# Re-ordering the steps of a fused linear-attention and rational-MLP kernel: a new table of steps, the same instructions

## The chip, the core and the metric

The kernel runs on one core of a Trainium2 chip. The metric is the device time of one execution in microseconds (us). Engines are named as the profile names them: PE is TensorE, with PEld its weight loads, DVE is VectorE, ACT is ScalarE, POOL is GpSimd, and SP is SyncE, which here only issues DMAs.

## The reference

Two stages are computed one after the other. The first is a gated linear recurrence over 768 time steps for 4 batches of 8 heads with head size 48. The second takes the 3072 x 384 result through a 2048-wide layer with a rational activation.

```python
f = 1.0 / (1.0 + np.exp(-f_logit))
for t in range(S):
    state = f[:, :, t, :, None] * state + np.einsum('bhd,bhe->bhde', k[:, :, t], v[:, :, t])
    y[:, :, t] = np.einsum('bhd,bhde->bhe', q[:, :, t], state)
...
h = x @ w_in
P = a[0] + a[1] * h + a[2] * h2 + a[3] * h3
Q = 1.0 + np.abs(b[0]) * np.abs(h) + np.abs(b[1]) * h2
g = P / (Q + 1e-06)
return (g @ w_out).astype(np.float32)
```

## The kernel before

The work is cut into 12 units, each of 256 time steps of one batch. Unit n belongs to batch n mod 4, so units 0 to 3 start the recurrence of the four batches, and unit n needs the state that unit n - 4 left. Within a unit the recurrence is done in its chunked form with matmuls, and the second stage follows on the unit's 256 tokens.

Every piece of work is a step with a short name. A step issues the instructions of one small function, and the text `ORDER` (lines 19 to 98) lists all 823 steps. The tile framework is in a mode in which it records exactly this order: each engine carries out its own instructions in the order of the text, and semaphores hold an instruction until its inputs are there and its output buffer is free. So the text sets the order within each of the five queues, and nothing else decides it.

The steps that the prediction speaks of, with their engines:

- `ld n f/k/q` loads inputs through SP's queue, and `ld n v` through POOL's (line 193). `wi 8 12` loads columns 8 to 11 (in blocks of 128) of `w_in` through POOL's queue (line 199). `>ls.1` holds a load until step `ls 1` has run.
- `cu`, `ci` build triangular constants and the identity on POOL. `cz`, `cm` clear or build constants on DVE. `fa` works out scale factors from `b` on DVE (from line 247), and `fb` scales `a`.
- `ef`, `ls` (ACT) take exp and log of the gates of a unit. `cs` (PE, line 286) sums them over time. `A` (ACT, line 302) takes exp of the sums, `A n 0` for q and `A n 1` for k. `xa n 0` and `xa n 1` (DVE, line 308) scale q and k with it.
- `T` (PE, line 320) transposes q and k, `Te` (ACT or DVE, line 332) copies the result out. `sc` (PE, line 345) forms the scores of one half of the heads, `mk` (DVE, line 353) masks them. `yb` and `yi` (PE, line 367) form the output `y`, and `ye` (ACT, or DVE for one third of unit 0) copies it into `xT`.
- `kv`, `si` (PE) form the new state, `ae` (ACT) its decay, `st` (DVE, line 445) writes it. `vm` (POOL, line 360) copies parts of v into a padded tile that `yb` needs.
- `h n m0 m1` (PE, line 454) multiplies `xT` with blocks m0 to m1 of `w_in`; `ha` and `hb` are the two parts of such a step. `hy` (ACT, or DVE once) copies the product out as bf16. `sq`, `ab`, `p1`, `p2`, `pm`, `gm` (DVE) and `ln`, `lz`, `ex` (ACT) form the rational function; `u` (PE) or `zd` (an adding DMA from POOL) forms the denominator, `ta` (an adding DMA) or `tv` (DVE) adds up the numerator.
- `o` (PE, line 567) multiplies with `w_out`, `oe` copies out, `so` stores.
- `dz k @s` issues k matmuls on constants (tile `warm`, line 295) whose result is not used; they keep PE busy.

`@s` names one of four PSUM slots of two banks each. Buffers for loads are three deep per input, so a load of unit n waits until the data of the unit three loads earlier has been read.

Of the kernel before, what the change touches and what calls it, by code (L numbers as in the profile page):

```python
# [19 lines left out]
ld 0 f 2 4; cu 1; cz 0; ab_ b a; ld 0 f 0 2; cz 2; ld 0 k 0 2; cu 0; ld 0 k 2 4; ld 0 q 2 4; ci; cm; dz 9 @0  # L20
ld 0 q 0 2; ld 1 f; ld 0 v; ab_ a s; ld 1 k; fa; ld 1 q; ef 0 2 4; ef 0 0 2; cz 3; ls 0 0 2; ls 0 2 4; cz 1
cs 0 2 4 @2; cs 0 0 2 @3; A 0 0 2 4; dz 4 @0; A 0 1 2 4; xa 0 0 2 4; A 0 1 0 2; xa 0 1 2 4; A 0 0 0 2
xa 0 1 0 2; T 0 2 4 @0; vm 0 1; kv 0 @3; Te 0 2 4; wi 8 12; xa 0 0 0 2; ae 0; sc 0 1 @0; si 0 0; mk 0 1
T 0 0 2 @2; ef 1; dz 5 @1; fr; Te 0 0 2; ld 2 f >mk.0.1; ls 1; ld 3 f; st 0 0; sc 0 0 @0; ld 2 k; cs 1 @2
# [5 lines left out]
pm 0 8 16; h 1 12 16 @1; ls 3; st 1 1; hy 0 4 8; p2 0 8 16; h 1 8 12 @0; hy 1 12 16; ab 0 4 8; sq 0 4 8  # L30
h 0 0 4 @2; hy 1 8 12; xa 2 1; ab 1 8 16; h 1 4 8 @3; ld 5 k; hy 0 0 4; ld 4 k; sq 1 8 16; ld 6 f; cs 3 @1
hy 1 4 8; ab 0 0 4; u 0 12 16 @2; xa 2 0; vm 2 0; A 3 1; ld 4 v; p1 0 0 8; T 2 @0; ln 0 12 16; ld 3 v; xa 3 1
u 0 8 12 @3; A 3 0; ta 0 8 16; sq 0 0 4; Te 2 s; h 1 0 4 @2; vm 2 1; xa 3 0; wo 8 12; ln 0 8 12; p2 0 0 8
sc 2 0 @0; kv 2 @1; ef 5; mk 2 0; si 2 0; ae 2; hy 1 0 4; sc 2 1 @3; st 2 0; yb 2 0 2 @0; ex 0 8 16; mk 2 1
# [591 lines left out]
```

## Time and profile before

| what | value |
|---|---|
| runs | 216.26, 216.90, 217.07 us; median 216.9 us |
| span of the profiled execution, first to last instruction | 214.4 us |
| PE busy | 201.0 us (94%) |
| DVE busy | 201.7 us (94%) |
| ACT busy | 195.8 us (91%) |
| POOL busy | 83.7 us (39%) |
| read from and written to HBM | 25.17 MB, 4.72 MB |

The profiled execution shows its span only. The median of the runs stands 2.5 us above that span, and this is taken as what lies around it. In what follows, a row of the timeline starts with the start and the duration in us, and ends with the idle time before it and what ended it. The first and last columns of a table by stretches are the stretch and the DMA rate; between them stand the busy times of the engines.

### The profile page before, as it was taken

To read this page: it belongs to the slowest core of one execution; us is meant where nothing else is said; L and a number is where in the kernel's file an instruction comes from. 1 tells how busy PE (TensorE), PEld (TensorE's weight loads), DVE (VectorE), ACT (ScalarE), POOL (GpSimd) and SP (SyncE) were. 2 spreads that over 40 slices of the span, in tenths; PEclk is the share of its full clock that TensorE was granted. 3 is DMA by queue.
4 is the path that set the end of the run, shared out by engine and by line. 5 is a ranking of instruction groups with operands and counts; after the bars stand their busy time and mean duration, and the time that the engine had idled before them with its cause. 6 is when DMAs were issued, how large, how long until landed. Compare 5 with 4: busy or idle time off the path is not lost.

```text
span 214.4 us, 7128 instructions
## 1 busy us (share of the span) xinstructions
PE 201.0 (94%) x3166; PEld 139.9 (65%) x3166; DVE 201.7 (94%) x213; ACT 195.8 (91%) x204; POOL 83.7 (39%) x93
## 2 busy tenths in 40 slices
PE   5875999899999999999999899999999999999993
PEld 1544587567767686586687587686577676776461
DVE  4786899999999999999999999999999999999991
ACT  3574689999999999999999999999999999999990
POOL 5161009009165072183270496696350603114200
PEclk9999999999999999999999999999999999999999
DMA  5999999999999999999999499999499896988823
GB/s 143 240 257 217 201 242 197 195 223 223 187 200 248 247 235 219 253 228 203 192 292 193 81 294 215 209 225 208 89 192 200 164 196 126 174 282 151 187 84 148
DMA packets 61199, 43.20 MB, mean 202 GB/s; under 512 B 51184, under 2 KB 55024, under 8 KB 61168
## 3 DMA queue, kind: packets, MB, share of 16 engines
q0 software_dynamic: 21520, 23.86, 67.3%
q1 hardware_dynamic: 39360, 18.68, 34.5%
q8 instruction: 25, 0.41, 0.8%
q10 hardware_dynamic: 288, 0.20, 0.3%
q14 instruction: 6, 0.05, 0.1%
HBM read 25.17 MB, written 4.72 MB: 139 GB/s over the span
## 4 chain that ended last, share of the span: by engine, by line
PE 39%; DVE 29%; ACT 14%; DMA 9%; issue 6%; SPq 2%; POOL 1%; DVEq 0%
PE hp L454 13%; PE op L567 12%; DVE gall L557 6%; DMA w_in_sb<-in_moe_w_in_dram 6%; DVE gall L545 4%; ACT qi L527 4%; ACT hy L484 4%; DVE z L497 3%; DVE h L489 3%; DVE scm L353 3%; DMA fn<-in_f_logit_dram 3%; PE u L505 3%; DVE gall L531 3%; PE y L367 2%; DVE hy L536 2%
## 5 line engine op out<-in xcount | busy, mean ns | idle before, releaser
L567 PE MATMUL op<-w_out_sb,gall 128*128 128x384 bf16 x384 | 69.2, 326 | 0.4 <-DVE gall L557 0.4
L454 PE MATMUL hp<-xT,w_in_sb 128*128 128x256 bf16 x564 | 66.7, 273 | 2.1 <-DMA w_in_sb<-in_moe_w_in_dram 2.0
L454 PEld LDWEIGHTS <-w_in_sb 128*128 128x128 bf16 x564 | 54.2, 98 | 11.5 <-DMA w_in_sb<-in_moe_w_in_dram 2.5
L567 PEld LDWEIGHTS <-gall 128*128 128x128 bf16 x384 | 36.1, 98 | 23.6 <-DVE gall L557 0.8
L484 ACT CAST hy<-hp 128x1024 bf16<-128x1024 f32 x47 | 48.1, 1076 | 2.3 <-PE hp L478 1.4
L527 ACT ACTIVATE qi<-lq 128x2048 bf16<-128x2048 f32 (+1 forms) x26 | 48.0, 1861 | 0.1
L360 POOL COPY vmp<-vn 128x128 bf16<-128x128 bf16 x24 | 35.2, 1516 | 28.4 <-DMA vn<-in_v_dram 22.7
L549 POOL DMA_DIRECT2D gall<-hy x20 | 20.0, 1068 | 53.9 <-ACT lsp L276 10.6
L523 ACT ACTIVATE lq<-z 128x2048 f32<-128x2048 bf16 (+1 forms) x20 | 36.8, 1874 | 0.0
L353 DVE TENSOR_TENSOR scm<-sc,mask 128x1024 bf16<-128x1024 f32 x24 | 29.0, 1215 | 1.9 <-PE sc L345 1.7
L489 DVE TENSOR_TENSOR h<-hy 128x4096 bf16<-128x4096 bf16 (+2 forms) x19 | 28.5, 1500 | 0.0
L557 DVE TENSOR_TENSOR gall<-gall,qi 128x4096 bf16<-128x4096 bf16 (+2 forms) x17 | 28.2, 1666 | 0.2
L545 DVE TENSOR_TENSOR gall<-gall,h 128x4096 bf16<-128x4096 bf16 (+2 forms) x17 | 28.1, 1652 | 0.0
L519 POOL DMA_DIRECT2D z<-h x17 | 19.3, 1366 | 17.0 <-PE u L505 6.0
L302 ACT ACTIVATE A<-cs 128x768 f32<-128x768 f32 (+1 forms) x26 | 19.4, 799 | 1.8 <-PE cs L286 1.8
L193 POOL DMA_DIRECT2D vn<-in_v_dram x12 | 12.4, 1030 | 15.7 <-PE y L367 7.9
L531 DVE TENSOR_SCALAR gall<-hy,a_sb 128x4096 bf16<-128x4096 bf16 (+1 forms) x14 | 16.9, 1208 | 0.0
L536 DVE TENSOR_SCALAR hy<-hy,a_sb 128x4096 bf16<-128x4096 bf16 (+1 forms) x14 | 16.6, 1185 | 0.0
L497 DVE TENSOR_SCALAR z<-hy 128x4096 uint16<-128x4096 uint16 (+2 forms) x19 | 15.7, 834 | 0.4 <-ACT hy L484 0.4
L330 ACT COPY qkT<-tp 128x1024 f32<-128x1024 f32 x11 | 11.6, 1058 | 3.2 <-PE tp L320 3.2
L320 PE MATMUL tp<-ident,qkp 128*128 128x128 bf16 x192 | 12.9, 219 | 0.8 <-DVE qkp L308 0.5
L320 PEld LDWEIGHTS <-qkp 128*128 128x128 bf16 x192 | 11.5, 98 | 2.5 <-DVE qkp L308 0.9
(73 smaller groups left out, 255.8 us busy)
## 6 DMA issues: line engine op xcount, KB each, us to landing
gall<-hy POOLq DMA_DIRECT2D x18, 512.0 KB, 7.1
z<-h POOLq DMA_DIRECT2D x15, 512.0 KB, 8.4
fn<-in_f_logit_dram SPq DMA_DIRECT2D x11, 384.0 KB, 8.5
kn<-in_k_dram SPq DMA_DIRECT2D x11, 384.0 KB, 12.1
qn<-in_q_dram SPq DMA_DIRECT2D x11, 384.0 KB, 11.3
out_dram<-osb SPq DMA_DIRECT2D x11, 384.0 KB, 5.1
vn<-in_v_dram POOLq DMA_DIRECT2D x12, 192.0 KB, 8.9
w_in_sb<-in_moe_w_in_dram POOLq DMA_DIRECT2D x4, 384.0 KB, 10.1
```

What stands on the lines that cost most here:

```text
L320: nc.tensor.transpose(t[:, x, i, p, :], s["qk"][:, i, x, 2 * p:2 * p + 2, :].rearrange("t h d -> t (h d)"), ident)
L353: return nc.vector.tensor_mul(t, s["sc", g].rearrange("s r a i t -> s (r a) (i t)"), mb)
L360: nc.gpsimd.tensor_copy(s["vm"][:, :, :, 32 * x:32 * x + 16], src)
L454: nc.tensor.matmul(t[:, m - m0, :], w_in_sb[:, kk, m * P:(m + 1) * P], s["x"][:, kk].rearrange("p i j t -> p (i j t)"), start=(kk == 0), s ...
L484: (nc.scalar.copy if eng == "s" else nc.vector.tensor_copy)(fl(big(s, "hy", "hy", 3), m0, m1), fl(s["hp", m0], 0, m1 - m0))
L489: return nc.vector.tensor_mul(fl(big(s, "h2", "h2", 2), m0, m1), fl(s["hy"], m0, m1), fl(s["hy"], m0, m1))
L523: nc.scalar.activation(fl(lq, m0, m1), fl(s["z"], m0, m1), AF.Ln, scale=regs[2], bias=1.0 + 1e-6)
L527: nc.scalar.activation(fl(qi, m0, m1), fl(lq, m0, m1), AF.Exp, scale=-1.0)
L531: return nc.vector.tensor_scalar(fl(big(s, "g", "gall", 3), m0, m1), fl(s["hy"], m0, m1), a_sb[:, 3:4], a_sb[:, 2:3], op0=ALU.mult, op1=AL ...
L545: return nc.vector.tensor_mul(fl(s["g"], m0, m1), fl(s["g"], m0, m1), fl(s["h2"], m0, m1))
L557: return nc.vector.tensor_mul(fl(s["g"], m0, m1), fl(s["g"], m0, m1), fl(qi, m0, m1))
L567: nc.tensor.matmul(s["op", j][:, j, 0:DM], s["g"][:, m, P * j:P * j + P], w_out_sb[:, m, :], start=(s["on", j] == 1), stop=(s["on", j] == KF))
```

## The change

Only the text `ORDER` changes. Both texts hold the same 823 steps with the same arguments, apart from the PSUM slots behind `@`; nothing is added, taken away or given to another engine. The new text has one line fewer, so every later line of the kernel has a number lower by one. The order is described as found by a search that moves steps within each engine's queue. Two lines of the text show its form; the second pair holds the same place in the work, the first product with `w_in`:

```diff
-ld 0 f 2 4; cu 1; cz 0; ab_ b a; ld 0 f 0 2; cz 2; ld 0 k 0 2; cu 0; ld 0 k 2 4; ld 0 q 2 4; ci; cm; dz 9 @0
+ld 0 f 2 4; ab_ b a; ld 0 f 0 2; ld 0 v; ef 0 2 4; ef 0 0 2; ls 0 0 2; cu 0; ld 0 k 2 4; fa; dz 5 @0; dz 9 @2
...
-Te 1 s; st 0 1; ab 0 8 12; ha 0 12 16 @0; ef 2; sc 1 1 @3; sc 1 0 @1; mk 1 1; ls 2; hb 0 12 16; cs 2 @2; ld 5 f
+sq 0 8 12; ab 0 8 12; ld 2 q; ha 0 12 16 @3; hb 0 12 16; sc 1 0 @0; vm 1 0; mk 1 0; ef 2; ld 2 v; ls 2
```

On PE the steps ahead of the first `cs` were `dz 9` and are now `dz 5` and `dz 9`; the five came later before, behind the second `T` of unit 0. SP's queue now has `ld 1 f` ahead of `ld 0 k 0 2` and `ld 0 q 0 2`, which stood ahead of it.

On DVE the first chain of the program, that of unit 0 up to its first `ye` (the tile `xT`), reads like this before; `qkp0` and `qkp1` are the scaled q and k of units 0 and 1, `scm` the masked scores:

```order
L235 MEMSET vmp1_95 128x8x8
L308 TENSOR_TENSOR qkp0_87<-qn_135,A_89 128x2x4x48
L308 TENSOR_TENSOR qkp0_87<-kn_127,A_89 128x2x4x48 x2
L332 COPY qkT_258<-tp_207 128x4x256
L308 TENSOR_TENSOR qkp0_87<-qn_135,A_89 128x2x4x48
L353 TENSOR_TENSOR scm1_282<-sc_264,mask_85 128x1024
L332 COPY qkT_258<-tp_284 128x4x256
L445 TENSOR_TENSOR state0_1_97<-sv_217,alast_262 128x384
L353 TENSOR_TENSOR scm0_334<-sc_309,mask_85 128x1024
L435 TENSOR_SCALAR xT_426<-y_340,sig_109 128x2x2x64
L308 TENSOR_TENSOR qkp1_88<-kn_161,A_89 128x2x8x48
L308 TENSOR_TENSOR qkp1_88<-qn_172,A_89 128x2x8x48
```

The same place on DVE reads like this in the new order:

```order
L241 MEMSET state3_0_102 128x192
L331 COPY qkT_216<-tp_205 128x4x256
L307 TENSOR_TENSOR qkp0_87<-kn_126,A_89 128x2x4x48
L307 TENSOR_TENSOR qkp0_87<-qn_184,A_89 128x2x4x48
L352 TENSOR_TENSOR scm1_243<-sc_223,mask_85 128x1024
L331 COPY qkT_216<-tp_291 128x4x256
L444 TENSOR_TENSOR state0_1_97<-sv_245,alast_287 128x384
L352 TENSOR_TENSOR scm0_382<-sc_314,mask_85 128x1024
L307 TENSOR_TENSOR qkp1_88<-qn_289,A_89 128x2x8x48
L434 TENSOR_SCALAR xT_419<-y_333,sig_109 128x2x2x64
L444 TENSOR_TENSOR state0_0_96<-sv_245,alast_287 128x384
L307 TENSOR_TENSOR qkp1_88<-kn_301,A_89 128x2x8x48
```

The clearing of the four state tiles (`cz 3`) moved from ahead of the chain to ahead of its first copy, the scaling of unit 1's q (`xa 1 0`) moved ahead of the `xT` row, and the second state of unit 0 (`st 0 1`) now stands right behind that row.

On POOL the first loads of v (`vn`) and of `w_in` stand like this before, with the copies into the padded tiles `vmp0` (even units) and `vmp1` (odd units):

```order
masks.py:199 AFFINE_SELECT ident_84<-ident_84 128x128
L193 DMA vn_158<-in_v_dram 128x8x96
L360 COPY vmp0_94<-vn_158 128x8x16
L199 DMA w_in_sb_110<-in_moe_w_in_dram 128x3x512 x2
L360 COPY vmp0_94<-vn_158 128x8x16
L193 DMA vn_355<-in_v_dram 128x8x96
L199 DMA w_in_sb_110<-in_moe_w_in_dram 128x3x512 x2
L193 DMA vn_445<-in_v_dram 128x8x96
L360 COPY vmp1_95<-vn_355 128x8x16 x2
```

In the new order the same place on POOL reads:

```order
masks.py:199 AFFINE_SELECT ident_84<-ident_84 128x128
L359 COPY vmp0_94<-vn_116 128x8x16 x2
L198 DMA w_in_sb_110<-in_moe_w_in_dram 128x3x512 x2
L192 DMA vn_312<-in_v_dram 128x8x96
L198 DMA w_in_sb_110<-in_moe_w_in_dram 128x3x512
L359 COPY vmp1_95<-vn_312 128x8x16
L198 DMA w_in_sb_110<-in_moe_w_in_dram 128x3x512
L359 COPY vmp1_95<-vn_312 128x8x16
L192 DMA vn_507<-in_v_dram 128x8x96
```

The load of unit 0's v left this place: it is now the first instruction of POOL's program, ahead of all constants. The fourth load of `w_in` (blocks 0 to 3) moved behind a copy that reads unit 1's v, and so does the load of unit 2's v.

More of the change, by code (lines that the diff above doesn't have):

```diff
@@ L19 @@
 ORDER = """
-ld 0 f 2 4; cu 1; cz 0; ab_ b a; ld 0 f 0 2; cz 2; ld 0 k 0 2; cu 0; ld 0 k 2 4; ld 0 q 2 4; ci; cm; dz 9 @0
[L21 to L24, printed above, removed]
@@ L30 @@
[L30 to L34, printed above, removed]
```

142 lines of the change are left out of this document (75 added, 67 removed).

## The prediction

> **What bounds the kernel now.** First I read busy time by stretches, because a mean over the program hides where an engine has room.
>
> ```profile
> core 0: us, PE busy (x) PEld busy (x) DVE busy (x) ACT busy (x) POOL busy (x), PEclk, DMA share, GB/s
> 0.00:25.10 25.10, 17.81 (x314) 10.73 (x314) 17.92 (x47) 13.23 (x21) 9.01 (x23) 1.00 1.15 212
> 25.10:35.00 9.90, 9.64 (x149) 7.74 (x149) 9.36 (x14) 8.61 (x11) 2.32 (x3) 1.00 1.15 225
> 35.00:199.30 164.30, 161.88 (x2639) 114.74 (x2636) 164.24 (x136) 164.01 (x163) 71.52 (x67) 1.00 1.05 204
> 199.30:214.40 15.10, 11.65 (x69) 6.67 (x69) 10.16 (x18) 9.91 (x12) 0.84 (x1) 1.00 0.47 139
> ```
>
> From 35 to 199 us DVE idles 0.06 us of 164.30, ACT 0.29 us and PE 2.42 us. The instructions stay the same, so an order cannot shorten this stretch: it can only put waits into it. All that can be won is DVE's idle time ahead of it, 7.18 us up to 25.1 and 0.54 us up to 35, and what lies in the tail. The tail I leave as it is: the same DVE steps follow `gm 10` in both texts, and so do the 64 matmuls of `o 10` and `o 11`, which with the last `u` fill most of PE's 11.65 us there.
>
> So the second view is the timeline of DVE in the head. The brackets give the idle time before a row and who ended it.
>
> ```profile
> 4.10 0.17 DVE L247 TENSOR_SCALAR bm<-b_sb 128x2 uint32<-128x2 uint32 x1 [0.73 <-DMA b_sb<-in_moe_b_dram]
> ...
> 5.59 0.84 DVE L242 MEMSET state<- 128x192 f32 x4
> ...
> 7.69 0.56 DVE L308 TENSOR_TENSOR qkp<-qn,A 128x384 bf16<-128x384 f32 x1 [0.78 <-ACT A L302]
> ...
> 13.00 1.23 DVE L353 TENSOR_TENSOR scm<-sc,mask 128x1024 bf16<-128x1024 f32 x1
> 14.86 0.48 DVE L435 TENSOR_SCALAR xT<-y,sig 128x256 bf16<-128x256 f32 x1 [0.64 <-PE y L367]
> 15.26 0.95 DVE L308 TENSOR_TENSOR qkp<-kn,A 128x768 bf16<-128x768 f32 x1
> 16.13 0.95 DVE L308 TENSOR_TENSOR qkp<-qn,A 128x768 bf16<-128x768 f32 x1
> 17.00 0.73 DVE L259 TENSOR_SCALAR a_sb<-a_sb,sig 128x3 f32<-128x3 f32 x3
> 18.33 1.23 DVE L484 CAST hy<-hp 128x1024 bf16<-128x1024 f32 x1 [0.60 <-PE hp L454]
> 19.47 0.55 DVE L445 TENSOR_TENSOR state<-sv,alast 128x384 bf16<-128x384 f32 x1
> 19.93 0.42 DVE L497 TENSOR_SCALAR z<-hy 128x1024 uint16<-128x1024 uint16 x1
> 22.09 1.23 DVE L353 TENSOR_TENSOR scm<-sc,mask 128x1024 bf16<-128x1024 f32 x1 [1.74 <-PE sc L345]
> 23.24 0.68 DVE L489 TENSOR_TENSOR h<-hy 128x1024 bf16<-128x1024 bf16 x1
> 23.84 1.22 DVE L353 TENSOR_TENSOR scm<-sc,mask 128x1024 bf16<-128x1024 f32 x1
> ```
>
> DVE waits 0.78 us for the first `A`, 0.64 for the first `y`, 0.60 for the first product with `w_in`, and 1.74 for unit 1's scores. The third view says what those waits hang on: the timeline of PE, and that of POOL, which issues the weights.
>
> ```profile
> 2.67 3.89 PE L295 MATMUL warm<-Ui 128*128 128x512 bf16 x9 [2.67 <-POOL Ui L218]
> 6.64 0.24 PE L286 MATMUL cs<-lsp,Ui 128*128 128x192 bf16 x1
> ...
> 7.30 1.03 PE L295 MATMUL warm<-Ui 128*128 128x512 bf16 x4
> ...
> 16.81 1.48 PE L454 MATMUL hp<-xT,w_in_sb 128*128 128x256 bf16 x12 [1.74 <-DMA w_in_sb<-in_moe_w_in_dram]
> 18.13 1.06 PE L320 MATMUL tp<-ident,qkp 128*128 128x128 bf16 x16
> 21.08 0.61 PE L478 MATMUL hp<-xT,w_in_sb 128*128 128x256 bf16 x4 [1.90 <-DMA w_in_sb<-in_moe_w_in_dram]
> ```
>
> ```profile
> 0.81 0.20 POOL masks.py:65 MEMSET Us<- 128x128 bf16 x1 [0.29 <-POOLq L610]
> ...
> 3.11 1.06 POOL L193 DMA_DIRECT2D vn<-in_v_dram  x1
> 9.40 0.28 POOL L360 COPY vmp<-vn 128x128 bf16<-128x128 bf16 x1 [5.23 <-DMA vn<-in_v_dram]
> 9.63 0.76 POOL L199 DMA_DIRECT2D w_in_sb<-in_moe_w_in_dram  x1
> 12.83 0.77 POOL L199 DMA_DIRECT2D w_in_sb<-in_moe_w_in_dram  x1 [2.44 <-ACT lsp L276]
> 13.60 0.30 POOL L360 COPY vmp<-vn 128x128 bf16<-128x128 bf16 x1
> 13.83 0.90 POOL L193 DMA_DIRECT2D vn<-in_v_dram  x1
> 14.72 1.50 POOL L199 DMA_DIRECT2D w_in_sb<-in_moe_w_in_dram  x2
> 16.21 0.90 POOL L193 DMA_DIRECT2D vn<-in_v_dram  x1
> 24.14 0.53 POOL L360 COPY vmp<-vn 128x128 bf16<-128x128 bf16 x2 [7.03 <-DMA vn<-in_v_dram]
> ```
>
> PE waits twice for weights, until 16.81 and until 21.08, and DVE's waits of 0.60 and 1.74 us follow from them. The chain of waits has a third such place:
>
> ```profile
> 14.72 12.03 DMA w_in_sb<-in_moe_w_in_dram
> ...
> 26.79 4.12 PE hp L454 x36
> ```
>
> The head is thus held by the arrival of `w_in`, whose first load POOL issues only at 9.63, after waiting 5.23 us for a v that it asked for at 3.11.
>
> **The change, part by part.** *The start gets later.* POOL now issues unit 0's v first, which takes 1.06 us; then `Ui` ahead of `Us`, where before both were built between 0.81 and 2.67, 0.93 us each. `Ui` is there at about 0.81 + 1.06 + 0.93 = 2.8, close to 2.67. But 14 idle matmuls, not 9, now precede the first `cs`. The nine took 3.89 us, the next four 0.26 us each, so 14 take 3.89 + 5 x 0.26 = 5.2 us, and `cs` starts at 8.0 and not at 6.64: 1.4 us later. So does DVE's first `xa`, at 9.1 and not 7.69.
>
> [...]
>
> *What DVE does meanwhile.* It starts with `fa`, which waits for `b` until 4.10 in either order and ended at 5.59; `cz 0`, `cm` and `cz 1` follow. `cz 1` took 0.5 us (from 5.59 + 0.84 to 7.69 less 0.78), `cz 0` clears as much, and for `cm` I allow 0.7, so they end near 7.3. Nothing fills 7.3 to 9.1. From the first `xa` to the end of the second `mk` the old order took 7.69 to 14.23 (13.00 + 1.23), 6.54 us with 0.24 of waiting for a transpose. The new order does the same 6.3 us and, in between, `cz 3` (0.84 us) and the small `cz 2` (0.2), which cover that wait: 9.1 + 7.3 = 16.4. That is 2.2 us behind.
>
> *Where it catches up.* From `ye` to the end of unit 1's second `mk`, the old order went from 14.86 to 25.06 (23.84 + 1.22): 10.2 us, of which 2.34 were the waits for `hy` and for `sc`, so 7.86 us of work. The new order puts `xa 1 0` (0.95) ahead of `ye`, which covers the 0.64 for `y`. `y` is there at 16.4 + 0.64 = 17.0, ACT copies its part, and `h 0 8 12` starts near 17.8; its result comes 1.52 us later (18.33 less 16.81), at 19.3. DVE has then done `xa`, `ye`, `st` and `xa`, until about 19.0, so 0.3 us of waiting remain. Next, PE ends `h` at 19.1 (1.32 us, 16.81 to 18.13), `T 1` at 20.2 and `ha` with `hb`, twelve matmuls like those of `h`, at 21.5; they now stand together ahead of `sc 1 0`. DVE has `hy`, `fb`, `sq` and `ab`, 1.23 + 0.73 + 0.68 + 0.42 less overlaps, until about 22.1, so the scores are ready in time. End of that stretch: 16.4 + 7.86 + 0.3 = 24.6 against 25.06, a lead of 0.5 us.
>
> This rests on `w_in` blocks 8 to 11 landing by 17.8 and 12 to 15 by 20.3. The v of unit 0 is asked for 2.3 us earlier (0.81, not 3.11), and both its copies run at once, so the first load goes out at about 7 and not 9.63. In the old order the first one landed 7.2 us after issue (9.63 to 16.81) and the second 8.25 us (12.83 to 21.08). The second still waits for `ls 1`; `ld 1 f` went ahead of two half loads, and `ls 1` went ahead of `ae 0` on ACT, so I put its issue at 12.2. Landing at 14.2 and at 17.9 to 20.5, they fit, the second by little.
>
> *Then* the third load issues 1 us earlier than 14.72, so the place at 26.79 moves forward as well. DVE has `st`, `sq`, `p1`, `ab`, `p2`, `pm` to do first, and I count its idle 0.54 us between 25.1 and 35 as gone. Lead: 0.5 + 0.54, about 1.1 us (24.6 is 24.55 before rounding), from 35 us on. PE gains about as much, since its two weight waits were 1.74 and 1.90 us and its start loses 1.4.
>
> *The middle.* The order of nearly every queue is a little different, with the same set of steps near each place. I looked for loads that got less time. Unit 6's v is now issued behind `zd 3 0 8`, unit 8's behind `zd 4 8 16`, and k of unit 9 behind a load that needs `xa 8 0`. The last one has ten DVE steps until `xa 9 1` reads it. These are the landing times by source over the whole program:
>
> ```profile
> DMA to landing us min/median/max: 5.5/8.9/16.3
> ```
>
> That is for v; the 8.9 fits and 16.3 would not. I take 0 for the middle and keep 1 us of loss for the range.
>
> Sum: 214.4 - 1.1 = 213.3 us of span, and with the 2.5 us between the span and the median of 216.9, **215.8 us**. A measurement of this kernel can tell about 0.5% (1.1 us) from no change, so this sits on that border.
>
> **The rivals.** *The fourth weight load comes too late: slower.* `wi 0 4` now stands behind a copy of unit 1's v. That v landed at 24.14, 10.3 us after its issue at 13.83, and the load itself was issued at 15.4 before. If the v still lands near 23.5, the load goes out at 24 and lands 7.1 to 10.1 us later, by the loads of `w_in`:
>
> ```profile
> DMA to landing us min/median/max: 7.1/10.1/13.9
> ```
>
> That is 31 to 34, while `h 0 0 4` started at 30.9 before. PE, in order, holds everything behind it, and no later stretch gives it back: 0 to 3.2 us more than before, 216.9 to 220, about 218.3 in the middle. It decides from a landing of the v after about 22. For it speaks the saturated DMA share of 1.15; against it, that POOL's loads now start 2.6 us earlier and queue behind each other. I give 0.20.
>
> *Nothing is left of the lead: no change.* The five extra idle matmuls run at 432 ns, or the first gates land late beside v, so that `cs` comes 0.9 us later still; or the middle takes back 1 us. 216.4 to 217.3. [...] I give 0.18.
>
> *More is won.* The weights arrive so early that neither `hy` nor `sc` nor anything up to 35 us waits. The upper bound is the old waits of 0.64 + 0.60 + 1.74 + 0.54 = 3.5 less the 1.4 of the later start, 2.1 us: 214.8. I give 0.17.
>
> **How the numbers follow.** The forecast's own case has 0.45, from 215.0 to 216.4; a little over half of it (0.25) lies beyond 1.1 us. Faster by over 0.5%: 0.25 + 0.17 = 0.42. Within 0.5%: 0.20 + 0.18 = 0.38. Slower: 0.20. The range takes in the larger gain with a little more, 214.3, and two fifths of the late-load case, up to 218.0.
>
> **What would show it.** Right: in the new profile the first `cs` starts at about 8, DVE's first `xa` near 9, unit 1's second `mk` ends near 24.6, no wait for `w_in` at the second and third products, and DVE again without idle time from 35 us on. Wrong: PE waiting for `w_in` near 31, a DVE idle time of over 1 us in the middle, or a first `cs` at 9 or later. If the span is shorter by much more than 2.1 us, the busy time of DVE itself must have changed, which my sum excludes.

## The result, and the profile after

| | old order | new order |
|---|---|---|
| median of the runs | 216.69 us (216.26 to 217.07) | 224.51 us (223.69 to 225.11) |
| span of the profiled execution | 214.4 us | 222.0 us |
| busy: PE, DVE, ACT | 201.0, 201.7, 195.8 us | 202.6, 202.4, 196.7 us |

The new order is slower: 1.0359 times the old one's time, with a 95% interval of 1.0322 to 1.0397. The forecast was 215.8 us, and its range ended at 218.0. Medians further on leave out four executions that the record marks as slow: one of the run with 28 pairs, one of nine idle matmuls with the old rest, and two of the clustered run (222.90 and 223.53 us). The engines do the same work in nearly the same busy time, so what came was idle time. The first view is again the busy time by stretches, with the same borders as before, except that the last one ends with the longer span:

```profile
0.00:25.10 25.10, 16.95 (x310) 10.34 (x311) 17.20 (x47) 11.17 (x18) 9.97 (x24) 1.00 1.12 202
25.10:35.00 9.90, 9.36 (x146) 7.65 (x146) 9.25 (x13) 9.32 (x13) 1.31 (x2) 1.00 1.35 225
35.00:199.30 164.30, 157.99 (x2591) 110.92 (x2598) 159.18 (x130) 159.17 (x159) 59.65 (x63) 1.00 1.02 196
199.30:222.00 22.70, 18.36 (x114) 10.89 (x113) 16.82 (x26) 17.06 (x17) 4.01 (x4) 1.00 0.62 165
```

DVE, the third of the busy times, idles 5.12 us from 35 to 199.3 us, where it idled 0.06. Up to 35 us it idles 8.55 us (7.72 in the old order), and from 199.3 us to the end 5.88 (4.94). With 0.8 us more of busy time this is the 7.6 us of the span, and two thirds lie in the stretch that the prediction set to zero. The timeline of DVE shows what ended its waits there:

```profile
9.73 0.56 DVE L307 TENSOR_TENSOR qkp<-qn,A 128x384 bf16<-128x384 f32 x1 [2.39 <-ACT A L301]
...
23.57 2.33 DVE L352 TENSOR_TENSOR scm<-sc,mask 128x1024 bf16<-128x1024 f32 x2
...
50.40 2.56 DVE L352 TENSOR_TENSOR scm<-sc,mask 128x1024 bf16<-128x1024 f32 x2 [0.89 <-PE sc L344]
69.14 1.23 DVE L352 TENSOR_TENSOR scm<-sc,mask 128x1024 bf16<-128x1024 f32 x1 [0.59 <-PE sc L344]
87.26 1.22 DVE L352 TENSOR_TENSOR scm<-sc,mask 128x1024 bf16<-128x1024 f32 x1 [0.38 <-PE sc L344]
95.09 1.35 DVE L530 TENSOR_SCALAR gall<-hy,a_sb 128x4096 bf16<-128x4096 bf16 x1 [0.48 <-PE op L566]
99.61 1.23 DVE L352 TENSOR_TENSOR scm<-sc,mask 128x1024 bf16<-128x1024 f32 x1 [0.98 <-PE sc L344]
118.52 1.23 DVE L352 TENSOR_TENSOR scm<-sc,mask 128x1024 bf16<-128x1024 f32 x1 [0.49 <-PE sc L344]
159.40 0.56 DVE L444 TENSOR_TENSOR state<-sv,alast 128x384 bf16<-128x384 f32 x1 [0.41 <-PE tp L319]
178.77 2.36 DVE L352 TENSOR_TENSOR scm<-sc,mask 128x1024 bf16<-128x1024 f32 x2 [0.28 <-PE sc L344]
190.41 1.34 DVE L530 TENSOR_SCALAR gall<-hy,a_sb 128x4096 bf16<-128x4096 bf16 x1 [0.28 <-PE op L566]
```

The nine waits from 35 us on are 4.8 of the 5.12 us, and all of them are for PE, mostly for scores. PE was late, so its own timeline is read next: the start, and the four longest idle times after 35 us.

```profile
3.40 5.21 PE L294 MATMUL warm<-Ui 128*128 128x512 bf16 x14 [3.40 <-POOL Ui L217]
...
50.09 0.27 PE L344 MATMUL sc<-qkT 48*64 48x128 bf16 x5 [0.89 <-issue]
56.84 0.23 PE L366 MATMUL y<-scm,vn 64*32 64x128 bf16 x2 [0.40 <-issue]
90.75 0.23 PE L366 MATMUL y<-scm,vn 64*32 64x128 bf16 x1 [1.41 <-issue]
175.91 1.15 PE L566 MATMUL op<-w_out_sb,gall 128*128 128x384 bf16 x6 [1.02 <-issue]
```

"issue" means that PE waited for nothing that the profile shows. Each of these pauses lies inside one step, between matmuls of the same kind whose inputs were there: 3.72 us together, and none of the sort in the middle of the old order. On POOL, the rival with the late weights can be read off:

```profile
8.72 0.53 POOL L359 COPY vmp<-vn 128x128 bf16<-128x128 bf16 x2 [3.99 <-DMA vn<-in_v_dram]
9.19 0.80 POOL L198 DMA_DIRECT2D w_in_sb<-in_moe_w_in_dram  x1
...
21.25 0.29 POOL L359 COPY vmp<-vn 128x128 bf16<-128x128 bf16 x1 [6.09 <-DMA vn<-in_v_dram]
21.49 0.78 POOL L198 DMA_DIRECT2D w_in_sb<-in_moe_w_in_dram  x1
```

Unit 1's v came at 21.25, the fourth load of weights went out at 21.49, and PE never waited for it.

**What the pauses have in common.** PE's matmuls come in pairs, a weight load and a matmul (3166 loads and 3157 matmuls have a record). If the 3166 pairs are numbered in program order from 0, the pauses (from one weight load to the next: 1.15, 0.66, 1.64 and 1.50 us) stand at pairs 735, 863, 1374 and 2779. These are 95, 95, 94 and 91 more than a multiple of 128. The page's list of DMA queues has a queue for instructions:

```profile
q8 instruction: 25, 0.41, 0.7%
```

25 transfers of 16 KB for 3166 pairs are one per 127 pairs. In the trace's DMA records, the transfer nearest to each pause ends between 0.8 us before the pause begins and 0.2 us after. So theory 1 was: PE's instructions come in blocks of 128 pairs, a new block is asked for when PE enters another, and where a block holds mostly small matmuls it is used up before the next is there. Theory 2 was that the order is simply too tight between the engines, theory 3 that the later start is handed on.

### The profile page after: what moved, and what is told of

It is laid out like the page before. It is cut to its first block, busy times and chain, and to the rows that moved or that the text cites. A ratio compares the mean times of both kernels' runs of the same rounds, so it can differ in the third digit from the quotient of the medians.

```text
span 222.0 us, 7109 instructions
## 1 busy us (share of the span) xinstructions
PE 202.6 (91%) x3157; PEld 139.8 (63%) x3166; DVE 202.4 (91%) x213; ACT 196.7 (89%) x204; POOL 74.9 (34%) x93
## 4 chain that ended last, share of the span: by engine, by line
PE 53%; ACT 19%; DVE 14%; issue 6%; DMA 4%; POOL 1%; POOLq 0%; ACTq 0%; DVEq 0%
PE op L566 18%; PE hp L453 15%; ACT qi L526 7%; ACT hy L483 5%; ACT lq L522 5%; PE y L366 4%; DMA fn<-in_f_logit_dram 4%; PE u L504 3%; PE warm L294 3%; PE tp L319 3%; DVE qkp L307 3%; DVE h L488 2%; DVE scm L352 2%; PE sc L344 2%; PE cs L285 2%
## 5 line engine op out<-in xcount | busy, mean ns | idle before, releaser
L566 PE MATMUL op<-w_out_sb,gall 128*128 128x384 bf16 x384 | 70.1, 326 | 1.4 <-issue 1.0
L483 ACT CAST hy<-hp 128x1024 bf16<-128x1024 f32 x47 | 47.5, 1042 | 3.1 <-PE hp L453 3.1
L526 ACT ACTIVATE qi<-lq 128x2048 bf16<-128x2048 f32 (+1 forms) x26 | 46.3, 1817 | 0.1
L359 POOL COPY vmp<-vn 128x128 bf16<-128x128 bf16 x24 | 24.3, 1256 | 28.4 <-DMA vn<-in_v_dram 28.4
L518 POOL DMA_DIRECT2D z<-h x17 | 20.9, 1349 | 30.8 <-DVE z L496 11.1
L192 POOL DMA_DIRECT2D vn<-in_v_dram x12 | 13.2, 1102 | 13.4 <-PE y L366 7.1
L270 ACT ACTIVATE fn<-fn 128x768 f32<-128x768 f32 (+1 forms) x13 | 10.5, 806 | 4.3 <-DMA fn<-in_f_logit_dram 4.3
```

The source lines that it names most:

```text
L359: nc.gpsimd.tensor_copy(s["vm"][:, :, :, 32 * x:32 * x + 16], src)
L483: (nc.scalar.copy if eng == "s" else nc.vector.tensor_copy)(fl(big(s, "hy", "hy", 3), m0, m1), fl(s["hp", m0], 0, m1 - m0))
L518: nc.gpsimd.dma_start(out=fl(s["z"], m0, m1), in_=fl(s["h2"], m0, m1), accum_op=ALU.add)
L526: nc.scalar.activation(fl(qi, m0, m1), fl(lq, m0, m1), AF.Exp, scale=-1.0)
L566: nc.tensor.matmul(s["op", j][:, j, 0:DM], s["g"][:, m, P * j:P * j + P], w_out_sb[:, m, :], start=(s["on", j] == 1), stop=(s["on", j] == KF))
```

## The experiments

**Shifting the blocks.** These runs put small pairs on constants on PE, where it waits anyway, and change nothing else. All later block ends then fall on earlier steps. The control adds a whole block of 128.

```diff
+    def dy(k, sl):
+        t = slot(sl, [P, 2, 512], F32, "warm")
+        for i in range(k):
+            r, e = slice(R * (i % 2), R * (i % 2) + R), 32 * (i // 2 % 4)
+            nc.tensor.matmul(t[e:e + 32, i % 2, 0:R], Ui[r, 0:32], Ui[r, 0:R], start=True, stop=True,
+                             skip_group_check=True)
...
-cs 0 2 4 @2; cs 0 0 2 @1; cz 1
+cs 0 2 4 @2; cs 0 0 2 @1; dy 72 @0; cz 1
```

The second run has `dy 28 @0` there. The third and fourth take the old order:

```diff
-h 0 8 12 @1
+dy 64 @0; h 0 8 12 @1
```

with `dy 128 @0` in the fourth.

> The new order with 72 pairs of a small weight load and a small matmul on constants put on PE at 9.2 us, where it waits 2 us anyway; nothing else moves. In the trace of the changed kernel PE's instructions are fetched in 25 transfers of 16 KB, one per 128 pairs, and four pauses of PE (1.15, 0.66, 1.64 and 1.50 us between two weight loads, at 48.9, 56.2, 89.1 and 174.4 us) stand at pair 735, 863, 1374 and 2779, which are all 91 to 95 more than a multiple of 128, each within 0.8 us of the end of such a transfer. Theory 1 (instruction blocks: the order puts the end of a block right behind dense runs of small matmuls): the shift moves every block boundary 72 pairs earlier in the program, to places where the blocks last longer; the four pauses go, at most one of about 1 us comes, and the time falls by 2 to 4.5 us, to 220.0 to 222.5. Theory 2 (the order is too tight between the engines, and the pauses are only where PE happens to stand): no change, 224.0 to 225.0. Theory 3 (the later start is handed on): no change, 224.0 to 225.0.

> The same with 28 pairs. By the times of the pairs in the trace, this shift puts boundaries where blocks are shortest (2.9 us from 152.2, 3.4 us from 43.5, 3.6 us from 165.5, 4.2 us from 13.1), while a fetch begins 0 to 5.5 us after the boundary and takes 1. Theory 1: as many or more pauses at other pairs, about 28 less than those of before modulo 128 (at 63 to 67), and 224.5 to 228. Theories 2 and 3: no change, 224.0 to 225.0.

> The old order with 64 such pairs on PE at 14.7 us, where it waits 2.08 us for weights anyway. In the old order no pause of PE stands at a block's end. Theory 1: boundaries move into blocks of 4.5 us (from 145.8) and 4.9 us (from 24.2); one to three pauses of 0.5 to 1.5 us appear and the time rises by 0.5 to 3 us, to 217.2 to 219.7. Theories 2 and 3: no change, 216.3 to 217.2.

> The old order with 128 such pairs at the same place, one whole block, so that all later boundaries fall on the same instructions as before: the control for the added work itself. All theories: no change, 216.3 to 217.4, of which up to 0.5 us is the added pairs running beyond the wait. A rise of over 1 us would say that the pairs themselves cost time and that the other three runs have to be read less that.

Measured, beside the old order's 216.44 us: 223.43 us with 72 pairs (ratio 1.0316, 1.0253 to 1.0379), 222.57 with 28 (1.0273, 1.0192 to 1.0354), 217.99 for the old order with 64 (1.0055, 1.0026 to 1.0083) and 220.98 with 128 (1.0188, 1.0126 to 1.0249). The times fit theory 1 only in part: 72 pairs gained 1.1 us and not 2 to 4.5, and 28 pairs gained where a loss was expected. The old order with 64 came out as theory 1 expected, 1.5 us slower and with three pauses, of 1.29, 0.69 and 0.89 us from weight load to weight load, at pairs 223, 478 and 1757 (95, 94 and 93). The control was no control, it lost 4.5 us. The timelines of PE say why. With 72 pairs one pause is left in the middle (the profile is of the fastest of the five executions, 221.12 us, 2.3 under the median):

```profile
47.25 0.24 PE L373 MATMUL y<-scm,vmp 64*32 64x128 bf16 x4 [1.49 <-issue]
```

With 28 pairs there are two:

```profile
49.93 0.38 PE L326 MATMUL tp<-ident,qkp 128*128 128x128 bf16 x4 [1.60 <-issue]
143.03 0.23 PE L373 MATMUL y<-qkT,state 128*32 128x128 bf16 x2 [0.81 <-issue]
```

The pause at 47.25 and the one at 49.93 both stand at pair 735, as one did without a shift, although there it was scores, and now it is y and a transpose. The other one stands at pair 2269, which is 93 more than a multiple of 128. So the pauses belong to the pair's number and not to the step. And in the control, the 128 pairs are themselves a block that runs out:

```profile
17.00 0.99 PE L302 MATMUL warm<-Ui 64*32 64x64 bf16 x102 [1.70 <-issue]
23.47 0.27 PE L327 MATMUL tp<-ident,qkp 128*128 128x128 bf16 x2 [3.28 <-issue]
```

They stand at pairs 223 and 351 (95 and 95). That a block's end can stop PE is shown by these, and the traces also show when. Take as margin the time from the end of a block's transfer to PE's last weight load before the block's end, with the first transfer counted to the end near pair 223, the second to 351, and so on. In the 20 profiles, 46 block ends have a margin of less than 1.2 us, and at each of them the time to the next weight load is 1.2 to 1.6 us less the margin. From 1.6 us on it no longer follows the margin, and the smallest margin in the old order is 1.65 us. Which blocks pause is still not to be foreseen from the order alone, since in the traces of the two orders a transfer began between 1.7 us before and 4.5 us after PE had reached the block end that precedes the one it serves.

**Which part of the order loses the time.** Two runs join the two orders near 30 us; the lines show the seam, first against the new text, then against the old one.

```diff
 h 1 4 8 @0; sq 0 4 8; st 1 1; xa 2 1; ab 0 4 8; wo 12 16; ld 4 f
-hy 1 8 12; sq 1 8 16; ls 3
+ld 4 q; ls 3; hy 1 8 12; ab 1 8 16; ld 5 k
...
```

```diff
 ab 0 4 8; sq 0 4 8; h 0 0 4 @2; hy 1 8 12; xa 2 1
-ab 1 8 16; h 1 4 8 @3; ld 5 k
+ld 3 v; vm 2 1; wo 8 12; vm 3 0
...
```

> The new order for its first 135 steps (to about 30 us), then all other steps in the old order. It gives the head of the new order with the middle and the tail of the old. In the traces the new head leaves DVE 1.3 to 1.5 us behind at 35 us. Theory 1 (pauses of PE at block ends, all in the new middle): those pauses are gone, and what is left is the head, 217.5 to 218.5. Theory 3 (the later start is the whole cause and is handed on): 222 to 224.5. Theory 2 (the middle is too tight): as theory 1, 217.5 to 218.5.

> The reverse: the first 131 steps of the old order (to about 30 us), then all others in the new order. The same number of PE instructions lies ahead of each later step as in the new order, so blocks end at the same steps. Theory 1: the four pauses at pairs 735, 863, 1374 and 2779 come again, 1.3 to 1.5 us of head is won back, 222.3 to 223.5. Theory 2: the same time, 222.5 to 224, but its loss lies in waits between engines, without pauses of PE at block ends. Theory 3: 216.5 to 217.5.

The new head with the old rest took 218.38 us (1.0103, 1.0065 to 1.0141, beside 216.38), the old head with the new rest 223.04 (1.0304, 1.0257 to 1.0351). So the head costs 2.0 us and the rest 6.7, both within what theory 1 expected; together they are 8.7, more than the 7.8 between the two orders, so the two parts do not simply add up. The stretch from 35 to 199.3 us, first for the new head with the old rest, then for the old head with the new rest:

```profile
35.00:199.30 164.30, 161.17 (x2628) 114.52 (x2634) 164.24 (x138) 163.31 (x163) 69.53 (x65) 1.00 1.04 205
```

```profile
35.00:199.30 164.30, 157.90 (x2591) 110.86 (x2598) 159.21 (x130) 159.03 (x159) 59.91 (x63) 1.00 1.01 195
```

DVE's idle time in the middle goes with the middle's order: 0.06 us and 5.09. The second run has its pauses at pairs 734, 862, 1374 and 2779 again, of 1.09, 0.64, 1.64 and 1.52 us. Theory 3, that the later start is handed on, is refuted.

**The new order without pauses.** To size what else the middle loses, two runs looked for a shift that leaves none: 112 pairs in the head, then 72 in the head and 44 ahead of unit 3's sums.

```diff
-cs 0 2 4 @2; cs 0 0 2 @1; cz 1
+cs 0 2 4 @2; cs 0 0 2 @1; dy 72 @0; cz 1
...
-h 0 8 12 @2; hy 0 8 12 v
+dy 40 @3; h 0 8 12 @2; hy 0 8 12 v
```

> The new order with 72 small pairs on PE at 9.2 us, where it waits, and 40 more at 17.6 us, where it waits again; 112 in all, so blocks end 112 pairs earlier in the program. By the times of the pairs, no block from 35 us on then lasts under 5.8 us. Theory 1: no pause of PE of over 0.6 us at a block end from 35 us on, and 219.0 to 221.0: what stays over the old order is the head, 1.4 us, and waits between the engines, 1.5 us or so. Theory 2: 223.5 to 225. Theory 3: 223.5 to 225, or more, since the pairs stand in the head.

```diff
+        for i in range({3: 44}.get(n, 0)):
+            r, e = slice(R * (i % 2), R * (i % 2) + R), 32 * (i // 2 % 4)
+            nc.tensor.matmul(t[e:e + 32, i % 2, 0:R], Ui[r, 0:32], Ui[r, 0:R], start=True, stop=True,
+                             skip_group_check=True)
         for i in range(2):
             for i0, U in ((0, Ui), (1, Ui if i else Us)):
```

> The new order with 72 small pairs on PE at 9.2 us, as in an earlier run, and 44 more ahead of unit 3's sums of gates, near 34 us: blocks end 116 pairs earlier in the program from there on, and by the times of the pairs no block after that lasts under 5.8 us. It is to show the new order without pauses of PE at block ends. Theory 1 with a share for waits between the engines: no pause of over 0.6 us at a block end after 35 us, DVE idle 1.5 to 2 us from 35 to 180 us (the new order had 5.1, the old one 0.06), and 219.5 to 221.0; with the pauses alone as cause of the middle it would be 218 to 219. Theory 2 (the pauses cost nothing by themselves): 223.5 to 225.

Both missed. The first took 225.46 us (1.0436, 1.0379 to 1.0494). PE waited 2.01 us for unit 2's gates until 25.82 and paused 1.76 us from 27.17 on (at pair 479, or 95), and from there the granted clock, the last column but two, was halved for a while:

```profile
27.00:34.00 7.00, 5.52 (x86) 3.54 (x69) 3.95 (x6) 2.98 (x5) 0.99 (x2) 0.51 1.40 218
```

With that, its time says little about the middle, where two pauses of over 0.6 us came as well (0.79 us at pair 735, 1.02 at 1502). The second took 222.66 us (1.0291, 1.0251 to 1.0332), 1.9 us less than the new order, and kept two pauses, at pairs 991 and 1502 (95 and 94):

```profile
58.15 0.38 PE L464 MATMUL hp<-xT,w_in_sb 128*128 128x256 bf16 x2 [0.66 <-issue]
91.22 0.40 PE L377 MATMUL y<-qkT,state 128*32 128x128 bf16 x14 [1.28 <-issue]
```

DVE idled 4.43 us from 35 to 180 us there, where 1.5 to 2 was expected. Pauses thus explain some of the middle and not all of it: with 72 pairs, where 1.49 us of pause was left, DVE still idled 3.01 us from 35 to 199.3 us.

**One block made short, and the same work spread.** 128 small pairs ahead of unit 9's sums, where a block ends, and then 16 ahead of each of eight units' sums, in the old order:

```diff
         t = slot(sl, [P, 2, 512], F32, "cs")
+        for i in range({9: 128}.get(n, 0)):
+            r, e = slice(R * (i % 2), R * (i % 2) + R), 32 * (i // 2 % 4)
+            nc.tensor.matmul(t[e:e + 32, i % 2, 0:R], Ui[r, 0:32], Ui[r, 0:R], start=True, stop=True,
+                             skip_group_check=True)
```

The second has `{4: 16, 5: 16, 6: 16, 7: 16, 8: 16, 9: 16, 10: 16, 11: 16}` there.

> The old order with 128 small pairs on constants put on PE in one place, ahead of unit 9's sums of gates, at 117.9 us, which is where one block of its instructions ends and the next begins; one block then holds little else and runs in about 1.7 us. All later blocks end at the same steps as in the old order. Theory 1 (a block that runs faster than the next one is fetched): besides the 1.7 us of work, one or two pauses of PE of 1 to 4 us in all right behind the cluster, and 218.5 to 222. Rival (only the work counts): 216.4 to 218.2, like the next run.

> The old order with the same 128 pairs spread: 16 ahead of the sums of gates of each of units 4 to 11, from 52 to 139 us. The work on PE is the same as in one cluster, and from 139 us on the blocks end at the same steps as in the old order. Theory 1: no block gets much shorter; at most one pause of 1 us where the blocks are shifted in between; 216.4 to 218. Rival (only the work counts): the same as the clustered run, within 0.5 us.

The cluster took 217.84 us (1.0064, 1.003 to 1.0099), inside the rival's range, and its profile has no pause at a block's end: the transfer had begun at 117.75 us, while PE waited for ACT until 119.28. The spread pairs took 219.14 us (1.012, 1.0074 to 1.0165), more than the cluster, which neither theory had expected, and that was the first sign of a second cost. The weight loads of the added pairs, in the view by line, with the idle time ahead of them behind the second bar:

```profile
L285 PEld LDWEIGHTS <-Ui 64*32 64x32 bf16 x128 | 1.6, 89 | 2.5 <-issue 2.4
```

In one group "issue" was 0.9 us. Of the 2.4 us in eight groups, 0.78 are a pause inside one of them (at pair 1757, or 93), and 0.42 a gap inside another. The rest stands ahead of groups: five of them follow wide matmuls (128 x 128 weights) and began after 0.10 to 0.32 us, and the three that follow small ones began without a gap. So a change from wide matmuls to small ones seemed to cost something.

**How often PE changes from wide to small matmuls.** The timeline of weight loads shows such a change, from products with `w_out` to y:

```profile
105.11 0.75 PEld L566 LDWEIGHTS <-gall 128*128 128x128 bf16 x5
106.17 0.10 PEld L366 LDWEIGHTS <-vn 64*32 64x32 bf16 x4 [0.32 <-issue]
```

From the last wide load to the first small one it takes 0.41 us (0.20 on the way back), where two wide ones in a row take 0.16. From products with `w_in` to small ones it is 0.31, where two in a row take 0.11. Counted in the two texts, the old order goes from wide to small 43 times and the new one 50 times; counted by the weight loads in the traces it is 47 and 55, of which 40 and 50 come after 35 us. In the new order, products with `w_out` stand between pieces of y more often. The last two runs change that number alone: nine steps `o` of four matmuls are moved into runs of small steps of the old order (52 changes), and `o` and `si` steps are taken out of such runs in the new order (38). The first lines are two of the nine places, the second two of the others.

```diff
-o 0 0 12 16; st 4 0; A 6 0
-yb 4 0 2 @1; ab 3 0 16; yb 4 2 4; oe 0 0 2 s
+st 4 0; A 6 0
+yb 4 0 2 @1; ab 3 0 16; yb 4 2 4; o 0 0 12 16; oe 0 0 2 s
...
-o 2 0 0 4; yb 6 2 4; Te 7 s; sq 5 0 16
+yb 6 2 4; o 2 0 0 4; Te 7 s; sq 5 0 16
```

> The old order with nine steps of four wide matmuls each (products with w_out of units 0 to 7) moved behind one or two of the small steps that followed them, so that runs of small matmuls (scores and y) are cut in two: PE changes 52 times from wide to small matmuls and not 43 times; the new order does so 50 times. In the traces a change from a product with w_out to y takes 0.41 us from weight load to weight load and the way back 0.19, where two of a kind in a row take 0.16 and 0.01; so each added change costs PE 0.43 us. Theory of the changes (they are the part of the middle that the pauses do not explain): PE is busy 3 to 4 us longer, which is over the 2.4 us that it idles from 35 to 199 us in the old order, DVE begins to wait for scores there, and the time rises by 1 to 3 us, 217.5 to 219.5. Rival (an order of steps costs PE nothing by itself): 216.2 to 217.0.

```diff
-o 4 0 8 12; zd 6 0 8; vm 9 0; A 10 1; yb 8 0 2
+zd 6 0 8; vm 9 0; A 10 1; yb 8 0 2
...
-yi 8 1; yi 8 0; ae 9
+yi 8 1; yi 8 0; o 4 0 8 12; o 4 1 0 4; o 4 1 4 8; ae 9
```

> The new order with the reverse done at nine places: products with w_out and the one matmul of a step si that stood between small steps go behind them, so PE changes 38 times from wide to small matmuls and not 50 times. Theory of the changes: PE needs up to 5 us less, and the time falls by 1.5 to 4 us against the new order, to 220.5 to 223.0, less where a longer run of small matmuls makes a block run out (pauses at block ends stay and may grow). Rival (only the pauses and the head count): 224 to 225.5.

With nine changes more, the old order took 220.05 us, 3.1 more than beside it (1.0122, 1.0059 to 1.0186). With twelve fewer, the new one took 223.65 (1.0291, 1.0221 to 1.0361), 0.9 less than it had, so the first was met and the second was not. The idle time ahead of small weight loads is what moved. In the old order:

```profile
L367 PEld LDWEIGHTS <-vn 64*32 64x32 bf16 x384 | 7.8, 90 | 4.7 <-issue 3.6
...
L345 PEld LDWEIGHTS <-qkT 48*64 48x64 bf16 x384 | 6.2, 106 | 5.7 <-issue 4.0 <-ACT qkT L330 0.9 <-DVE qkT L332 0.6
L414 PEld LDWEIGHTS <-qkp 64*64 64x64 bf16 x384 | 4.2, 109 | 2.1 <-issue 1.1 <-DMA vn<-in_v_dram 0.6 <-DVE qkp L308 0.2
...
L367 PEld LDWEIGHTS <-state 128*32 128x32 bf16 x240 | 3.5, 95 | 3.1 <-issue 2.4 <-DVE state L445 0.4
```

The same four groups in the old order with nine changes more:

```profile
L367 PEld LDWEIGHTS <-vn 64*32 64x32 bf16 x384 | 7.9, 90 | 6.1 <-issue 5.4
...
L345 PEld LDWEIGHTS <-qkT 48*64 48x64 bf16 x384 | 6.3, 106 | 6.4 <-issue 4.5 <-ACT qkT L330 1.2 <-DVE qkT L332 0.6
L414 PEld LDWEIGHTS <-qkp 64*64 64x64 bf16 x384 | 4.2, 109 | 2.2 <-issue 1.7 <-DVE qkp L308 0.3
...
L367 PEld LDWEIGHTS <-state 128*32 128x32 bf16 x240 | 3.7, 95 | 4.7 <-issue 3.3 <-DVE state L445 1.0
```

"issue" adds up to 11.1 us and 14.9: 3.8 more, or 0.42 for each of the nine (0.39 from 35 us on; 0.3 us lie ahead of that, where the granted clock was 0.50 for a while in the second execution). In the new order the four come to 16.3, of which about 3.2 us are three of the pauses. With twelve changes fewer they are 13.2, about 3.5 of that pauses, so the changes did get cheaper by some 3.4 us. DVE's waits at 87.26, 118.52 and 159.40, quoted above, were gone, and its idle time from 35 to 199.3 us fell from 5.12 to 3.94 us. Part of what was not gained lies in the pauses, of which two grew (2.07 us instead of 1.64 at pair 1374, 1.66 instead of 1.50 at 2779), and in a start that came half a microsecond later in that execution (first scaling at 10.21, not 9.73). Where the rest went is not shown.

**The head.** Six runs ask what the head lost, and whether its idle time could be won. First the five idle matmuls are put back where they were, in the new order and in the new head with the old rest:

```diff
-fa; dz 5 @0; dz 9 @2
+fa; dz 9 @2
...
-T 0 0 2 @0; si 0 0
+T 0 0 2 @0; si 0 0; dz 5 @2
```

> The new order with one step moved: the five idle matmuls of the start stand again behind the second transpose of unit 0, as in the old order, so that nine stand ahead of the first sums of gates and not fourteen. In the new order those sums began at 8.66 us although their input was there at 6.9. Theory of the head (the fourteen hold the start by 1.7 us, and the load of unit 2's gates, which waits for the first masked scores, with it): first sums at 6.9, first scaling on DVE at about 8, unit 1's second masked scores end near 24.4, and the time falls by 1.2 to 1.8 us against the new order, to 222.5 to 223.5; the four pauses of PE at block ends stay at the same pairs. Rival (the head is held by the loads, so an earlier start waits for them): 224 to 225.

> The first 135 steps in the new order but with nine idle matmuls, all later steps in the old order: the head that the prediction priced, without its late start and without the new middle. Theory of the head: 1.2 to 1.8 us less than the same with fourteen idle matmuls (218.4), 216.3 to 217.2; if the lead that the prediction counted on is real (1.1 us at 35 us, and 1.4 more for the earlier start), as low as 214.5, faster than both orders. Rival (the loads hold it): 217.5 to 218.5.

Then unit 0's loads are issued as in the old order, in addition to that:

```diff
-ld 0 f 2 4; ab_ b a; ld 0 f 0 2; ld 0 v; ef 0 2 4
+ld 0 f 2 4; ab_ b a; ld 0 f 0 2; ld 0 k 0 2; ld 0 k 2 4; ld 0 q 2 4; ld 0 q 0 2; ld 1 f; ef 0 2 4
...
-cu 1; ci; cz 0
+cu 1; ci; ld 0 v; cz 0
```

> The new order with nine idle matmuls at the start, and with unit 0's loads issued as in the old order: f, k, q of unit 0 ahead of unit 1's f, and v behind the constants. With nine idle matmuls alone, the first scaling on DVE waited 1.44 us for q and began at 8.6 us, and the scores came 1.1 us late twice. Theory (the order of the first loads holds the new head): first scaling at 7.7 to 8.0 with no wait for q, unit 1's second masked scores end near 24.4 where the new order had 25.9, and 221.8 to 223.0. Rival (something else in the head is late, and the time does not move): 223.2 to 224.5.

> The same head (new order for the first 135 steps, nine idle matmuls, unit 0's loads as in the old order), then the old order. Theory of the loads: it keeps the gain that the prediction saw in the new head and none of its costs, 215.0 to 216.3. Rival: no gain is left, 216.4 to 217.5.

Nine idle matmuls gave 223.79 us (1.0318, 1.0272 to 1.0365), 0.7 less than the new order. With the old rest they gave 218.21 (1.0065, 1.0034 to 1.0097), 0.2 less than with fourteen. The timeline of DVE in the first of these runs:

```profile
8.60 0.56 DVE L307 TENSOR_TENSOR qkp<-qn,A 128x384 bf16<-128x384 f32 x1 [1.44 <-DMA qn<-in_q_dram]
...
13.46 1.23 DVE L352 TENSOR_TENSOR scm<-sc,mask 128x1024 bf16<-128x1024 f32 x1 [1.10 <-PE sc L344]
```

The start came 1.1 us earlier and then waited for q, so the loads hold it too. With the old loads as well it was 223.74 (1.0347, 1.0304 to 1.0390), and 217.88 with the old rest (1.0071, 1.0037 to 1.0104). One wait that is gone with the old loads shows in the new order on ACT and on PE:

```profile
23.78 0.84 ACT L270 ACTIVATE fn<-fn 128x768 f32<-128x768 f32 x1 [1.47 <-DMA fn<-in_f_logit_dram]
```

```profile
25.55 0.32 PE L285 MATMUL cs<-lsp,Ui 128*128 128x384 bf16 x1 [1.69 <-ACT lsp L275]
```

These are unit 2's gates. SP issued their load at 14.61 us and not at 11.91 as in the old order, and ACT, which waited for them, was late with a decay that DVE then waited for: 0.61 us at 26.51, and 1.20 in the new head with the old rest. With nine idle matmuls and the old loads, DVE began at 7.72 us in the new order, as in the old one, and still waited 0.70 and 0.95 us for unit 0's scores; with the old rest it was 1.10 us twice. The old order had no such wait. So about 1.4 us of the head's 2.0 stay with the rest of its order; these waits are the likeliest place, but no run took them away.

Two runs tried to win idle time in the old head: the first load of weights ahead of the copy of v, and unit 1's scores ahead of the matmuls that wait for the second load.

```diff
-vm 0 1; kv 0 @3; Te 0 2 4; wi 8 12
+wi 8 12; vm 0 1; kv 0 @3; Te 0 2 4
```

> The old order with one step moved: the first load of weights for the first product (columns 8 to 11) goes ahead of the copy of v that it stood behind, so POOL issues it at about 4.2 us and not at 9.63, where it waited 5.23 us for v. Theory of the head (the arrival of the weights holds it): the load lands near 12 to 13, PE's wait until 16.8 goes, DVE's 0.60 us for the first product goes and part of its 1.74 us for the scores; 214.5 to 216.2. Rival (the load only takes transfer time from f, k and q of unit 0, which hold the start): 216.4 to 218.

```diff
-ha 0 12 16 @0; ef 2; sc 1 1 @3; sc 1 0 @1; mk 1 1
+sc 1 1 @3; sc 1 0 @1; ha 0 12 16 @0; ef 2; mk 1 1
```

> The old order with unit 1's scores put ahead of the four matmuls that wait for the second load of weights until 21.08 us. In the old order DVE waits 1.74 us for these scores behind that load. Theory of the head (idle time of DVE before 35 us is what can be won, since DVE has none after it): the scores are formed at 20.3, right behind the copied transposes, DVE's wait falls to 0.5 to 0.9 us and the kernel gets 0.5 to 1.2 us faster than the old order, 215.2 to 216.0. Rival (PE or ACT then waits the same, and the gain is lost before 35 us): 216.2 to 216.8.

The first was slower, 217.88 us (1.0058, 1.0031 to 1.0085), as its rival had it: PE waited 1.65 us for unit 1's gates, and DVE 2.62 us for the first y, where it had waited 0.64. The second took 216.13 beside 216.49 (0.9983, 0.9965 to 1.0001), 0.36 less where 0.5 to 1.2 was expected, and not clear of no change. Its timeline of DVE:

```profile
20.79 1.23 DVE L353 TENSOR_TENSOR scm<-sc,mask 128x1024 bf16<-128x1024 f32 x1 [0.41 <-PE sc L345]
...
25.10 0.56 DVE L445 TENSOR_TENSOR state<-sv,alast 128x384 bf16<-128x384 f32 x1 [1.35 <-ACT alast L441]
```

and of PE:

```profile
23.94 0.44 PE L414 MATMUL sv<-vn,qkp 64*64 64x48 bf16 x32 [0.91 <-DMA vn<-in_v_dram]
```

The wait of 1.74 us for scores fell to 0.41, and the next one, which had been 0.23 us, became 1.35. It hangs on unit 1's v, which lands near 24 us in either case. The gain was lost to a new wait.

## Why the prediction was wrong, point by point

*The start gets later: right, and a little short.* The first `cs` came at 8.66 us (forecast 8.0), the first `xa` at 9.73 (9.1). The fourteen matmuls took 5.21 us against 5.2; constants came 0.6 us later than worked out. The first load of `w_in` went out at 9.19 and not at 7, because v was asked for at 1.34 and not at 0.81, took 7.4 us to land and not 6.3, and the two copies ahead of the load took 0.5. That the five matmuls alone made it late was wrong: without them the loads hold the start.

*Where it catches up: wrong.* Unit 1's second `mk` ends at 25.90 us (23.57 + 2.33), not at 24.6. PE indeed no longer waited for weights, but the lead of 1.1 us became a loss: 2.0 us, from the run that joins the new head to the old rest. Of the 1.3 us, 0.7 are there when unit 0's second `mk` ends (17.07 and not 16.4); from there to 25.90 DVE waits 0.63 us where 0.3 was allowed, and its work takes 0.3 longer. Then DVE waits 0.61 us more at 26.51, behind unit 2's gates, a load that the prediction did not follow. The step that failed was to count idle time as winnable because the wait named ahead of it went. In the run with unit 1's scores put forward, another input, due at the same time, took its place.

*The middle at 0, with 1 us kept for the range: wrong, and the step that decided.* DVE idles 5.12 us there, which the prediction had named as a sign of being wrong (over 1 us), and the middle with the tail costs 6.7 us. The prediction said rightly that an order can only put waits into a stretch in which DVE idles 0.06 us. It then looked only at loads, and took each step's own time as fixed. Two costs of PE that depend on the neighbours of a step were missing: a change from wide to small matmuls (about 0.4 us by the run with nine more), and the end of a block of 128 pairs, where PE was there less than 1.2 us after the block's transfer had ended (46 such ends in the 20 profiles).

The pauses at block ends are 3.72 us of PE's time. For the changes, the four groups of small weight loads give 2.0 us, 1.6 of it from 35 us on: 16.3 us of "issue" less 3.2 of pauses is 13.1, against 11.1 in the old order. Together that is near DVE's 5.12 us, and DVE's own waits show both. 2.9 us of them come behind pauses (0.89, then 0.48 and 0.98, then 0.28 and 0.28); with 72 pairs, which left one pause, only a wait of 1.50 us behind that pause stood in their place. The waits of 0.38, 0.49 and 0.41 us stayed with 72 pairs (0.38, 0.32 and 0.41) and were gone with twelve changes fewer. The 0.59 at 69.14 fell to 0.20 with 72 pairs and stayed with fewer changes, so its place is open. The split is an estimate, as the parts push each other: fewer changes made two pauses longer. No run took both costs away. The runs that took away a part of one won 0.9 to 1.9 us each, apart from the one with 112 pairs, whose clock was halved for a while. In the old order, which had none of these pauses, each cost was put in alone: shifting its blocks by 64 pairs cost 1.5 us, and nine changes more cost 3.1.

The size of such a block is read from the trace of the new order: 25 transfers of 16 KB for 6332 instructions of pairs, and pauses whose distances are multiples of 128 pairs, within four. A block's end cost up to 3.28 us in the lines above, in the run with 128 pairs.

*The tail as it is: short.* DVE idles 0.94 us more there.

*The 2.5 us around the span: about 0.8 too much.* The executions on record stand 1.6 to 1.9 us above their own spans, and the rest is that the profiled execution was shorter than the median one. The sum takes the 2.5 over from the old order's median, so the forecast does not suffer from it.

*The rivals.* The late fourth load did not decide: its load did go out behind v, at 21.49 us, but v landed before 22. The middle taking back 1 us, one of the cases of the no-change rival, had the right place and under a fifth of the size. No rival had an engine losing time of its own between two steps.

*What stays open:* 1.4 us of the head, the exact split of the middle, and why a transfer of instructions begins up to 4.5 us after PE has reached the block end that precedes the one it serves. That a search on a replay of a trace would not see either cost, if it gives each step a fixed time, is an argument and not shown.

## What to carry to other kernels

Where an engine is busy 98% of a stretch, price a new order by what its neighbours cost, not only by waits: count the changes between kinds of matmul, and look for blocks of 128 pairs that would run in a few microseconds (in the new order the four that ended in a pause took 4.3 to 6.1 us up to it, and one of 4.8 us did not pause). A pause put down to "issue" inside a run of equal instructions may be a question of where it stands in the program, so number the instructions, and set the pause beside the transfers of instructions. And an idle time is won only if the next input is early as well: check what lands next before you count it.

## What the runs showed of the hardware that was not expected

- PE can pause at the ends of blocks of 128 pairs, 91 to 95 more than a multiple of 128. In 11 of the 20 orders profiled such a pause of over 0.9 us was seen. At all 46 block ends where the transfer had ended less than 1.2 us before PE's last weight load, the time to the next one was 1.2 to 1.6 us less that margin (in the new order, margins of 0.24, 0.80 and 0.09 us gave 1.15, 0.66 and 1.50).
- A change from 128 x 128 weights to small tiles took 0.41 us from load to load behind products with `w_out` and 0.31 behind those with `w_in`, the way back 0.20.
- In the run with 112 pairs the granted clock was 0.50 for 6.8 us from 27.17 us on, where a pause of 1.76 us begins. What brings it about is not shown: it was 0.50 for 3.4 us from 16.8 us on in the old order with nine changes more, and 1.00 at that place in the old order.
